# Moving four FP32 matmuls from ahead of a value chunk into three waits of the same chain

## The chip, the cores and the metric

One core of one Trainium2 chip. The metric is the device time of one execution of the whole kernel in microseconds (us). A run gives one such time; where a kernel ran several times, its median stands with its lowest and highest. Spans and the times inside a trace count from the first instruction of the profiled execution and end about 1.7 us below the device time of the same execution (667.5 against 669.24 for the kernel before). In the lines of the profile PE is the tensor engine (TensorE), PEld its weight loads, DVE VectorE, ACT ScalarE and SP the engine that issues the DMAs; L634 is line 634 of the kernel.

All runs of this study count as one state; no run was more than 1.5% above the fastest of its kernel. Below that limit the executions differ by more than the change can give (668.22 to 669.44 us over 48 runs of the kernel before), and much of this document is about that.

## The reference

A block of attention with a key and value cache, followed by a two-layer MLP, both with a modulated layer norm. Batch 8, one query position, D = 512, 32 query heads on 8 key heads of 128, 8,192 cached positions, F = 1,792, all bf16. The code here is condensed.

```python
def _A_ref(x, k_cache, v_cache, wq, wo):            # attention
    q = (x @ wq).reshape(B, Sq, Hq, Dh).transpose(0, 2, 1, 3)
    k, v = jnp.repeat(k_cache, rep, axis=1), jnp.repeat(v_cache, rep, axis=1)
    p = _softmax(jnp.einsum('bhqd,bhkd->bhqk', q, k) * Dh ** (-0.5))
    o = jnp.einsum('bhqk,bhkd->bhqd', p, v)
    return o.transpose(0, 2, 1, 3).reshape(B, Sq, Hq * Dh) @ wo
def _B_ref(x, w1, b1, w2, b2):                      # MLP
    h = jnp.einsum('bsd,df->bsf', x, w1) + b1
    r = jnp.where(h > 0, h, 0)
    return jnp.einsum('bsf,fd->bsd', r * r, w2) + b2
...                                                  # sa, ca, ga, sb, cb, gb from c and w_mod
h = _layernorm(x) * (1 + ca) + sa
x = x + ga * _A_ref(h, k_cache, v_cache, wq, wo)
h = _layernorm(x) * (1 + cb) + sb
x = x + gb * _B_ref(h, w1, b1, w2, b2)
```

## The kernel before

For each of the 8 batches the kernel reads four key units and four value units of 4 MB through a ring of four slots. Only the end matters here. The very last value unit comes in chunks, and the MLP weights follow it on the same queue, `w1` in two parts and `w2` in four:

```python
d_w1 = [dma("sync", s_w1[i], ...) for i, (a, z) in enumerate(((0, 3), (3, 4)))]
d_w2 = [dma("sync", s_w2[i], ...)
        for i, (a, z, j) in enumerate(((0, 4, 4), (4, 8, 4), (8, 12, 4), (12, 14, 2)))]
```

Most of the output projection is done early, before the last value unit is complete, in four column groups of the PE array. Their four partial sums must be added; that is done by `partial`, four FP32 matmuls with a selection matrix, into the same PSUM tile in which the last quarter of the projection is summed later:

```python
def partial(ks):
    for k in ks:
        op("tensor", lambda e, k=k: e.matmul(
            attn_ps[:, k, :], proj[:, 128 * k:128 * (k + 1)], SELP[:, :],
            start=(k == 0), stop=False, skip_group_check=True), [k_proj])
...
k_proj = op("vector", lambda e: e.tensor_copy(proj, bank(7)), [proj_done])
... # biases of the MLP (L704, L707)
partial(range(0, 4))                                               # L697, the group
t = values(16, CH[1] // 4, 22)                                     # L634, second chunk
osb = O_sb[:, 1, :]
t = op("vector", lambda e: e.tensor_copy(osb, bank(3)), [t])       # L713, the cast
direct(CH[1], CH[2], 2)                                            # L690 x16, third chunk
for i in range(4):
    op("tensor", ... e.matmul(oT_ps, osb[:, i * 128:(i + 1) * 128], SEL[:, i, :], ...), [t, k_all])   # L716
t = direct(CH[2], CH[3], 3)                                        # L690 x8, fourth chunk
t = op("vector", ... e.tensor_tensor(oTn_p[...], oT_ps, rinv_p[...], ALU.mult), [t])  # L720, the division
k_oP = permute(...)                                                # L522 and four copies
for g in (6, 7): ...                                               # L727, rest of the projection
```

After that come the residual, the second layer norm, the first MLP layer (L754) and the second (L769). L769 is 56 matmuls in order; from the 33rd on they read the third part of `w2`, from the 49th on the fourth. Line numbers after the change are higher by 2 to 4: L634 becomes L636, L690 L692, L697 L699, L716 L718, L727 L731, L754 L758, L769 L773.

Of the kernel before, what the change touches and what calls it, by code (L numbers as in the profile page):

```python
# [33 lines left out]
class Prog:  # L34
# [19 lines left out]
    def op(self, eng, fn, deps=()):  # L54
        o = Op(eng, fn, deps, None, self.at)
        o.tok = Tok(o, self.at)
        self.ops[eng].append(o)
        return o.tok
# [110 lines left out]
def bass_adaLN_cond__gqa_block_cached__dense_activation_squared_relu__decode_kernel(  # L169
# [17 lines left out]
    with ExitStack() as es:  # L187
# [67 lines left out]
        oP = KF[:, 3008:3072].rearrange("p (g j b) -> p g j b", g=2, j=4)  # L255
# [11 lines left out]
        bank = lambda i: PS[:, i, :]  # L267
# [40 lines left out]
        t = pool(lambda e: e.memset(SELB[:], 0.0))  # L308
# [6 lines left out]
        t = select(IDENT[:], [[-1, 128]], 0, 1, 1.0, NE, t)  # L315
        t = select(IDF8[:], [[-1, 8]], 0, 1, 1.0, NE, t)
# [3 lines left out]
        t = pool(lambda e: e.memset(EYEB[:], 0.0))  # L320
        t = select(EYE[:], [[-32, 4], [-1, B]], 0, 1, 1.0, NE, t)
        t = k_eye = select(EYEB[:], [[-32, 4], [-1, B]], 0, 1, 1.0, NE, t)
        k_q0 = pool(lambda e: e.memset(QTm[:], 0.0))
        t = pool(lambda e: e.memset(Pm[:], 0.0), [t])
        k_pm = t
        for d in (-96, -64, -32, 0, 32, 64, 96):
            t = select(R4[:], [[-1, 128]], -d, 1, 1.0, NE, t)
        t = select(Qmask[:], [[-32, 4]], 0, 1, 0.0, GE, t)
        t = select(Qmask[:], [[32, 4]], 31, -1, 0.0, GE, t)
        for d in (0, 32, 64, 96):  # L330
            t = select(R4m[:], [[-1, 32]], -d, 1, 0.5, NE, t)

        for i in range(4):
            for cg in range(4):
                for half in range(2):
                    t = select(SEL[:, i, 4 * half:4 * half + 4], [[-1, 4]], -(32 * cg + 8 * i + 4 * half), 1,
                               1.0, NE, t)

        t = pool(lambda e: e.memset(SELP[:], 0.0), [t])
        for j in range(4):  # L340
            t = select(SELP[:], [[-1, B]], -40 * j, 1, 1.0, NE, t)
        t = select(PERM[:], [[-1, 4], [0, 4], [-4, 32]], 0, 1, 1.0, NE, t)
        t = select(SELB[:], [[-1, 4], [0, B]], 0, 1, 1.0, NE, t)
        t = pool(lambda e: e.memset(oTn[:], 0.0), [t])
# [31 lines left out]
        for k in range(KT):  # L376
            t = op("tensor", lambda e, k=k: e.matmul(csT_ps[:, k, :], cs_k[:, k, :], IDENT[0:B, 0:B],
                                                    is_transpose=True), [k_cs, k_id])
# [3 lines left out]
        for k in range(KT):  # L382
            t = op("tensor", lambda e, k=k: e.matmul(xT_ps[:, k, :], x_sb[:, k * 128:(k + 1) * 128],
                                                    IDENT[0:B, 0:B], is_transpose=True), [d_x])
        k_xT = op("vector", lambda e: e.tensor_copy(xT[:], xT_ps), [t])
        t = op("vector", lambda e: e.bn_stats(stats[:], x_sb), [d_x])
        t = op("vector", lambda e: e.bn_aggr(mv[:], stats[:]), [t])
        t = op("vector", lambda e: e.tensor_scalar(std_[:], mv[:, 1:2], EPS, None, ALU.add), [t])
        t = op("scalar", lambda e: e.activation(std_[:], std_[:], ACT.Sqrt), [t])
        t = op("vector", lambda e: e.reciprocal(rstd[:], std_[:]), [t])  # L390
        t = op("vector", lambda e: e.tensor_scalar(hn, x_sb, mv[:, 0:1], rstd[:, 0:1], ALU.subtract, ALU.mult), [t])
# [18 lines left out]
        t = row_groups(bank(0), csT, wmod_v, (0, 1), [k_csT, d_wm])  # L410
        k_mr0 = op("vector", lambda e: e.tensor_copy(mod_r[0:64, 0, :], bank(0)[0:64, :]), [t])
        t = row_groups(bank(1), csT, wmod_v, (2, 3, 4, 5), [])
        released[2] = t
        k_mr1 = op("scalar", lambda e: e.activation(mod_r[:, 1, :], bank(1), ACT.Copy), [t])
        for i in range(KT):
            t = op("tensor", lambda e, i=i: e.matmul(
                mod_ab[:, :, i, :], mod_r[0:64, 0, :].rearrange("r (p i) -> r i p", i=KT)[:, i, :],
                EYE[0:64, 0:2, :]), [k_mr0, k_xT])
# [51 lines left out]
        def pe_stream(n, at):  # L470
            rhs = IDENT[:, :].unsqueeze(1).to_broadcast([128, 4, 128])
            ts = [op("tensor", lambda e: e.matmul(  # L472
                bank(at).rearrange("p (a r) -> p a r", a=4), IDENT[:, :], rhs)) for _ in range(n)]
            return ts[0]
# [41 lines left out]
        hT_ps = [bank(i)[:, 0:16 * n].rearrange("p (f a b) -> p f a b", f=n, a=2) for i, n in enumerate((8, FT - 8))]  # L516
        yT_ps = bank(2)[:, 0:KT * B].rearrange("p (k b) -> p k b", k=KT)

        def permute(pP, q0, q1, dst, deps, fill):
            n = q1 - q0  # L520
            for j in range(4):
                t = t_act = op("tensor", lambda e, j=j: e.matmul(  # L522
                    pP[:, j, 0:64 * n].rearrange("p (h x) -> p h x", h=2), PERM[:, j, :, :].rearrange("p h m -> p (h m)"),
                    oTn_p[:, :, q0:q1, :, :].rearrange("p h q r b -> p h (q r b)"), start=True, stop=True), deps)
            if fill:
                t_act = pe_stream(fill, 4)
            toks = []
            for hl in range(REP):
                rows = slice(32 * hl, 32 * (hl + 1))
                dst_h = dst[rows, :, :, :]  # L530
                frm = pP[rows, :, 0:64 * n].rearrange("p j (x r b) -> p r x j b", x=2 * n, b=B)[:, hl]
                if hl % 2:
                    toks.append(op("scalar", lambda e, dst=dst_h, frm=frm: e.activation(dst, frm, ACT.Copy), [t_act]))  # L533
                else:
                    toks.append(op("vector", lambda e, dst=dst_h, frm=frm: e.tensor_copy(dst, frm), [t]))
            return toks
# [10 lines left out]
        for b in range(B):  # L547
# [76 lines left out]
            for p in range(NP):  # L624
# [47 lines left out]
                else:  # L672
# [15 lines left out]
                    def direct(a, z, i):  # L688
                        for m in range(a, z):
                            t = op("tensor", lambda e, m=m: e.matmul(  # L690
                                oT_w, vt[:, m, :], wide(lhs[:, NP - 1, 8 * m:8 * m + 8]), start=(m == CH[1]),
                                stop=(m == CH[3] - 1), skip_group_check=True), [got[i], k_rinv] + pmd[m // 32])  # L692
                        return t
# [8 lines that stand above are left out]
                    for hh, (f0, n, a, z) in enumerate(((0, 4, 0, 2), (0, 4, 2, 3), (4, 2, 3, 4))):  # L702
# [4 lines left out]
                    op("tensor", lambda e: e.matmul(  # L707
                        yT_ps, b2_row, SELB[:, :, :], start=True, stop=False, skip_group_check=True),
                        [s_bank_free[2]])
                    partial(range(0, 4))  # L710
                    t = values(16, CH[1] // 4, 22)
                    osb = O_sb[:, 1, :]
                    t = op("vector", lambda e: e.tensor_copy(osb, bank(3)), [t])  # L713
                    direct(CH[1], CH[2], 2)
                    for i in range(4):
                        op("tensor", lambda e, i=i: e.matmul(  # L716
                            oT_ps, osb[:, i * 128:(i + 1) * 128], SEL[:, i, :], start=False, stop=False,
                            skip_group_check=True), [t, k_all])  # L718
                    t = direct(CH[2], CH[3], 3)
                    t = op("vector", lambda e: e.tensor_tensor(  # L720
                        oTn_p[:, :, NP - 1, :, B - 1], oT_ps.rearrange("p (h r) -> p h r", h=2),
                        rinv_p[:, :, NP - 1, :], ALU.mult), [t])
                    k_oP = permute(bank(6)[:, 0:256].rearrange("p (j c) -> p j c", c=64), 3, 4, oP, [t], 0)
                    for g in (6, 7):
                        for j in range(4):
                            for k in range(KT):
# [97 lines left out]
```

## Time and profile before

| kernel before, first runs | |
|---|---|
| time, 3 runs | 668.8 us (668.22 to 669.38) |
| time of the profiled execution | 669.24 us, span 667.5 us |
| mean granted PE clock in it | 0.915 |
| the group (L697) | 8 records on PE, 0.99 us |
| last transfer lands (fourth part of `w2`) | 663.63, which is 3.88 us before the end of the span |

"Lands" is the semaphore record of the last of the 16 DMA engines of a transfer. A PE clock of 0.5 is half of the full one; the FP32 loads of the moved matmuls then follow each other at 0.21 us instead of 0.11, as read below. The lines are shown in the prediction, where each is read. One row should be kept in mind: the profiled execution took 669.24 us, above two of the three runs, and I took its trace for the kernel as it usually is.

### The profile page before, as it was taken

How to read it: one execution, taken by the hardware profiler on the slowest of the kernel's cores; microseconds unless marked ns; L12 is line 12 of the kernel's file. 1: busy time of each engine (PE TensorE's matmuls, PEld its weight loads, DVE VectorE, ACT ScalarE, POOL GpSimd, SP SyncE). 2: the span in 40 equal slices, each digit the busy share in tenths (PEclk: the TensorE clock that was granted, in tenths of full speed). 3: DMA queues.
4: the chain of work that ended last, by engine and by line, in shares of the span. 5: the costliest groups of instructions: out<-in, count | busy, mean ns of one | idle time of the engine just before them, and what ended most of it. 6: DMA issues, size and time to landing. Idle time of an engine off the chain costs nothing.

```text
span 667.5 us, 15923 instructions
## 1 busy us (share of the span) xinstructions
PE 524.1 (79%) x7259; PEld 351.0 (53%) x7259; DVE 308.1 (46%) x587; ACT 264.6 (40%) x307; POOL 20.5 (3%) x79
## 2 busy tenths in 40 slices
PE   3309988899839987599758988499776998489886
PEld 2107753675328742477316753287434773177535
DVE  2105662566316652267415662167513673146633
ACT  2104661466105651166314661156512663146611
POOL 7400000000000000000000000000000000000000
PEclk9658999899969999699998999799996999979996
DMA  9999999999999999999999999999999999999996
GB/s 374 438 408 438 431 418 433 436 432 426 434 434 432 428 434 434 430 430 434 434 430 428 436 434 428 430 436 432 428 432 436 430 428 434 436 430 426 434 419 263
DMA packets 12188, 283.85 MB, mean 425 GB/s; under 512 B 1260, under 2 KB 1296, under 8 KB 3600
## 3 DMA queue, kind: packets, MB, share of 16 engines
q1 hardware_dynamic: 12128, 283.65, 99.1%
q8 instruction: 9, 0.15, 0.1%
q10 hardware_dynamic: 48, 0.02, 0.0%
q14 instruction: 3, 0.02, 0.0%
HBM read 283.66 MB, written 0.01 MB: 425 GB/s over the span
## 4 chain that ended last, share of the span: by engine, by line
PE 59%; DMA 29%; ACT 7%; DVE 3%; issue 1%; POOL 0%; ACTq 0%; SPq 0%; DVEq 0%; POOLq 0%
PE PS L488 39%; DMA ring<-in_A_k_cache_dram 22%; PE PS L505 10%; DMA wo_sb<-in_A_wo_dram 7%; ACT P_sb L580 5%; PE PS L634 4%; PE PS L478 2%; ACT KTb L493 1%; DVE O_sb L654 1%; PE PS L472 1%; PE PS L592 1%; DVE Pm L606 1%; PE PS L612 0%; PE PS L541 0%; PE PS L658 0%
## 5 line engine op out<-in xcount | busy, mean ns | idle before, releaser
L488 PE MATMUL PS<-IDENT,ring 128*128 128x128 bf16 x4096 | 266.4, 227 | 64.6 <-DMA ring<-in_A_k_cache_dram 37.0
L488 PEld LDWEIGHTS PS<-IDENT,ring 128*128 128x128 bf16 x4096 | 245.9, 102 | 112.8 <-issue 49.6
L493 ACT ACTIVATE KTb<-PS 128x1024 bf16<-128x1024 bf16 x192 | 196.8, 1025 | 237.6 <-PE PS L488 237.6
L495 DVE COPY KTb<-PS 128x1024 bf16<-128x1024 bf16 x320 | 210.0, 688 | 153.8 <-PE PS L488 151.8
L505 PE MATMUL PS<-KTb,Qb 128*32 128x512 bf16 x1024 | 78.8, 384 | 4.5 <-ACT KTb L493 4.5
L634 PE MATMUL PS<-ring,Pm 128*32 128x512 bf16 x1018 | 64.6, 396 | 20.8 <-DMA ring<-in_A_v_cache_dram 20.0
L654 DVE CAST O_sb<-PS 128x512 bf16<-128x512 f32 x31 | 21.4, 692 | 105.8 <-PE PS L634 105.8
L634 PEld LDWEIGHTS PS<-ring,Pm 128*32 128x32 bf16 x1018 | 26.1, 99 | 55.8 <-DMA ring<-in_A_v_cache_dram 28.4
L533 ACT ACTIVATE KTb<-PS 32x192 bf16<-32x192 f32 (+1 forms) x18 | 5.6, 311 | 109.9 <-PE PS L472 103.1
L580 ACT ACTIVATE P_sb<-PS,negm 128x1024 bf16<-128x1024 f32 x32 | 35.2, 1113 | 20.2 <-DVE negm L575 20.2
L478 PE MATMUL PS<-ONES 128*128 128x512 f32 x80 | 42.1, 630 | 0.0
L472 PE MATMUL PS<-IDENT 128*128 128x512 bf16 x112 | 33.4, 380 | 0.0
L592 PE MATMUL PS<-IDENT,P_sb 128*128 128x128 bf16 x256 | 19.9, 220 | 15.4 <-ACT P_sb L580 15.4
L606 DVE COPY Pm<-PS 64x512 bf16<-64x512 bf16 x48 | 20.2, 421 | 25.0 <-PE PS L592 24.6
L592 PEld LDWEIGHTS PS<-IDENT,P_sb 128*128 128x128 bf16 x256 | 14.4, 98 | 25.2 <-ACT P_sb L580 25.2
L505 PEld LDWEIGHTS PS<-KTb,Qb 128*32 128x32 bf16 x1024 | 15.4, 94 | 21.0 <-ACT KTb L493 8.5
L512 DVE TENSOR_REDUCE m<-PS 128x1 f32<-128x512 f32 x32 | 22.1, 689 | 6.6 <-PE PS L505 6.6
L658 PEld LDWEIGHTS PS<-SEL,O_sb 128*128 128x128 bf16 x124 | 5.8, 97 | 29.4 <-DVE O_sb L654 29.4
L478 PEld LDWEIGHTS PS<-ONES 128*128 128x128 f32 x80 | 12.7, 190 | 10.6 <-issue 10.6
L658 PE MATMUL PS<-SEL,O_sb 128*128 128x8 bf16 x124 | 7.9, 169 | 12.3 <-DVE O_sb L654 12.0
L472 PEld LDWEIGHTS PS<-IDENT 128*128 128x128 bf16 x112 | 9.9, 103 | 10.1 <-issue 7.2
L541 PE MATMUL PS<-wo_sb,KTb 128*32 128x512 bf16 x192 | 11.8, 380 | 3.4 <-ACT KTb L533 3.4
(134 smaller groups left out, 146.5 us busy)
## 6 DMA issues: line engine op xcount, KB each, us to landing
ring<-in_A_k_cache_dram SPq DMA_DIRECT2D x32, 4096.0 KB, 31.4
ring<-in_A_v_cache_dram SPq DMA_DIRECT2D x31, 4096.0 KB, 27.5
ring<-in_A_wq_dram SPq DMA_DIRECT2D x1, 4096.0 KB, 19.8
wo_sb<-in_A_wo_dram SPq DMA_DIRECT2D x1, 4096.0 KB, 46.7
ring<-in_w_mod_dram SPq DMA_DIRECT2D x1, 3072.0 KB, 10.5
ring<-in_A_v_cache_dram SPq DMA_DIRECT2D x1, 2048.0 KB, 22.3
ring<-in_B_w_dram SPq DMA_DIRECT2D x3, 512.0 KB, 19.1
ring<-in_B_w_dram SPq DMA_DIRECT2D x1, 1344.0 KB, 17.6
```

Source lines behind the costliest of these rows:

```text
L472: ts = [op("tensor", lambda e: e.matmul(bank(at).rearrange("p (a r) -> p a r", a=4), IDENT[:, :], rhs)) for _ in range(n)]
L478: ts = [op("tensor", lambda e: e.matmul(bank(at).rearrange("p (a r) -> p a r", a=4), ONES[:, :], rhs)) for _ in range(n)]
L488: t = op("tensor", lambda e, j=j, i=i: e.matmul(STG[j][:, i, :], src[:, 32 * k + 8 * j + i, :], IDENT[:, :], is_transpose=True), [loaded[n ...
L493: stg_free[j] = op("scalar", lambda e, j=j, dst=dst: e.activation(dst, STG[j], ACT.Copy), [t])
L495: stg_free[j] = op("vector", lambda e, j=j, dst=dst: e.tensor_copy(dst, STG[j]), [t])
L505: t = op("tensor", lambda e, hf=hf, q=q, rhs=rhs: e.matmul(PS[32 * q:32 * (q + 1), k, :], Qb[:, 2 * p + hf, :], rhs, start=(p == 0 and hf ...
L512: return op("vector", lambda e: e.tensor_reduce(m4[:, k:k + 1], bank(k), AX.X, ALU.max), [t])
L580: exps.append(op("scalar", lambda e, k=k: e.activation(P_sb[:, k, :, :, :], bank(k).rearrange("p (i x) -> p i x", i=8).unsqueeze(2).to_bro ...
L592: t = op("tensor", lambda e, k=k, i=i: e.matmul(STG[k][:, i, :], P_sb[:, k, i, :, :].rearrange("p h x -> p (h x)"), IDENT[:, :], is_transp ...
L606: done.append(op("vector", lambda e, dst=dst, frm=frm: e.tensor_copy(dst, frm), [t, k_pm]))
L634: t = op("tensor", lambda e, m=m, cg=cg, p=p, vt=vt, Obank=Obank: e.matmul(Obank[32 * cg:32 * (cg + 1), :], lhs[:, p, 32 * m:32 * m + 32], ...
L654: t = op("vector", lambda e, osb=osb, Obank=Obank: e.tensor_copy(osb, Obank), [t])
```

## The change

The four matmuls of `partial` are taken away from in front of the last unit's second chunk. One is put behind the issue of the cast, one behind the fourth chunk's matmuls (while the division runs), two behind the permutation's matmuls (while its four copies run). The intent is that PE does them while it waits for VectorE and ScalarE anyway.

```diff
-        def permute(pP, q0, q1, dst, deps, fill):
+        def permute(pP, q0, q1, dst, deps, fill, then=None):
...
+            if then is not None:
+                then()
             toks = []
...
-                    partial(range(0, 4))
                     t = values(16, CH[1] // 4, 22)
                     osb = O_sb[:, 1, :]
                     t = op("vector", lambda e: e.tensor_copy(osb, bank(3)), [t])
+                    partial((0,))
                     direct(CH[1], CH[2], 2)
...
                     t = direct(CH[2], CH[3], 3)
+                    partial((1,))
                     t = op("vector", lambda e: e.tensor_tensor(
...
-                    k_oP = permute(bank(6)[:, 0:256].rearrange("p (j c) -> p j c", c=64), 3, 4, oP, [t], 0)
+                    k_oP = permute(bank(6)[:, 0:256].rearrange("p (j c) -> p j c", c=64), 3, 4, oP, [t], 0,
+                                   lambda: partial((2, 3)))
```

> **What bounds the kernel now.** I read the page first, then the end in the chain of waits, then the weight loads and the DMA queue in order of time. From the page:
>
> ```profile
> span 667.5 us, 15923 instructions
> DMA  9999999999999999999999999999999999999996
> ...
> L634 PE MATMUL PS<-ring,Pm 128*32 128x512 bf16 x1018 | 64.6, 396 | 20.8 <-DMA ring<-in_A_v_cache_dram 20.0
> ```
>
> The 16 DMA engines are busy in all 40 slices but the last, and the value matmuls (L634) idle almost only for the value cache's transfers. The eight passes are bound by what they read; the instructions at issue run once, after the last pass. So the question is what sets the end. The chain of waits, from 651 to 666 us:
>
> ```profile
> 652.97 0.99 PE PS L697 x8
> 653.96 0.77 PE PS L634 x10
> 654.73 0.02 issue
> 654.75 0.70 DVE O_sb L713
> 655.46 0.05 issue
> 655.50 0.26 PE PS L716 x4
> 655.76 0.23 PE PS L690 x8
> ...
> 656.01 0.20 DVE oTn L720
> 656.21 0.05 issue
> 656.25 0.30 PE PS L522 x4
> ...
> 657.18 1.01 PE PS L727 x32
> ...
> 662.86 1.66 PE PS L769 x56
> ```
>
> L697 is the group to be moved. It stands on this chain with 0.99 us, and everything after it follows in one line of compute; no DMA is named. But a chain names only what was last. How long before that the data had landed is not in it, so I took each transfer's issue and its time to landing from the queue's timeline and the DMA view, one short window each:
>
> ```profile
> 627.73 0.43 SPq L364 DMA_DIRECT2D ring<-in_A_v_cache_dram  x1
> ring<-in_A_v_cache_dram SPq DMA_DIRECT2D x1, 1280.0 KB, 25.2
> ...
> 628.69 0.42 SPq L364 DMA_DIRECT2D ring<-in_A_v_cache_dram  x1
> ring<-in_A_v_cache_dram SPq DMA_DIRECT2D x1, 256.0 KB, 26.1
> ...
> 648.55 1.60 SPq L680 DMA_DIRECT2D ring<-in_B_w_dram  x1
> ring<-in_B_w_dram SPq DMA_DIRECT2D x1, 512.0 KB, 14.4
> ...
> 650.21 0.88 SPq L680 DMA_DIRECT2D ring<-in_B_w_dram  x1
> ring<-in_B_w_dram SPq DMA_DIRECT2D x1, 256.0 KB, 13.4
> ```
>
> Start of issue plus time to landing: the value unit's second chunk lands at 627.73 + 25.2 = 652.9 us (652.88 in the trace's semaphore records, which have two decimals; I use those below), the fourth at 654.8 (654.75), the third part of the second MLP weight at 663.0 (663.00), its fourth and last at 663.6 (663.63). By the same reading the third chunk lands at 654.06 and the first MLP weight at 658.09 and 659.23. The users come very shortly after, as the weight loads show:
>
> ```profile
> 653.88 0.33 PEld L634 LDWEIGHTS PS<-ring,Pm 128*32 128x32 bf16 x10
> 655.59 0.27 PEld L690 LDWEIGHTS PS<-Pm,ring 128*128 128x128 bf16 x8
> ```
>
> The reader should set 653.88 against 652.88, and 655.59 against 654.75: the stream of data and the stream of compute run side by side here, compute less than 1 us behind.
>
> [...] the first L634 load stands at 653.88, right after the last L697 load (653.67 + 0.19), although its data was there at 652.88. So program order is what is paid for, and moving the group moves its time. [...] an L697 load (128x128 f32) takes 0.19 us and the loads follow each other at 0.11 us, those of L690 (bf16) take 0.096 us and follow at 0.025 us. [...] the trace has two records for each of the four matmuls (x8)[...]. [...] The four matmuls keep their order [...]; correctness can only be seen in the run.
>
> **The change part by part.** It adds no work and removes none: four FP32 matmuls (8 records) are placed one after L634, one after L690's last, two after L522. The vector and scalar instructions and transfers are the same. Ahead of L634 the eight records hold PE from 652.90 (first load) to 653.88 = 0.99 us; that is what is offered. In their new places:
> (a) The first (2 records: one step of 0.11 us and the last load, 0.21 us until the next bf16 load = 0.32 us) goes under the cast L713, 0.69 us. Before, 16 L690 loads at 0.025 us = 0.4 us ran there and PE then idled 0.29 us.
> (b) The second, 0.32 us, goes between the last L690 load (655.77) and the first L522 load (656.25), a gap of 0.48 us while L720 works. Fits.
> (c) The last two (3 x 0.11 + 0.21 = 0.54 us) go between L522's last load (656.32) and L727's first (657.15), 0.83 us while the four copies work. Fits.
> So the new places are free, with 0.16 us to spare at the least. Now the walk with landings. What a landing costs to the load it frees I take from a true wait earlier: landed 499.07, load at 499.11, so 0.04 us.
> 1. L634 may load at 652.88 + 0.04 = 652.93 instead of 653.88: gain 0.96 us, nearly all.
> 2. Cast ends 0.96 earlier, at 654.49. The first moved matmul follows the last L634 load and ends its hold at about 654.0; L690's sixteen need the third chunk, 654.06 + 0.04 = 654.10, and are through at 654.5. L716 can start at 654.54, when the cast allows. Gain still 0.96.
> 3. L690's last eight would start at 654.63 but need the fourth chunk: 654.75 + 0.04 = 654.79 against 655.59. Gain cut to 0.80.
> 4. L720, L522, copies, L727, the layer norm and L754 keep 0.80. L754 would load at 658.66, its weight is there at 658.09 and 659.23 (the last quarter is used from 660.25). L769 starts at 662.06 instead of 662.86.
> 5. L769's 56 loads run at 0.027 us. Its 33rd stood at 663.71, its 49th at 664.14. With a gain of 0.80 they would stand at 662.91 and 663.34, but the third weight part is there at 663.04 and the fourth at 663.67. Gain cut to 0.67 and then to 664.14 - 663.67 = 0.47.
> 6. What follows is fixed work: the last eight matmuls, the gate, the residual, output.
> Sum: 0.99 offered, 0.03 + 0.16 + 0.33 = 0.52 taken by three landings, **0.47 us** left, 0.07% of 668.8. Predicted time 668.8 - 0.5 = **668.3 us**.
>
> **The rivals.**
> A. The whole 0.99 us comes through (667.8). For it: the chain names no DMA at the end. Against it: the landings above. It holds only if the transfers end earlier in the new kernel, and nothing in the change moves an issue: the MLP weights wait for L658 of an earlier value unit, at 640.3.
> B. The new places aren't free and the chain takes back part (668.3 to 668.8). For it: place (b) has only 0.16 us to spare, and FP32 loads at half clock take longer (L750, 0.29 us each instead of 0.19). The granted clock falls to 0.50 at 656.84 in this trace, after place (c) in the new schedule, but that moment need not be the same in every execution. [...] Against it: the 0.33 us that the last landing takes anyway would hide that.
> C. The landing itself differs between executions, so that either all or nothing of the gain shows. The three times of before are spread over 1.16 us, more than twice the gain, so a median of three may lie on either side.
> D. A clock that is lost earlier[...]. The tail's small matmuls hardly notice: L716 at full clock is spaced 0.026 us, L727 at half clock 0.026 us. [...]
>
> **Range and chances.** Median expected at 668.3. The walk gives 667.8 at best and 668.8 if all is lost; the spread of before, about 0.6 us to each side, and the state of another chip come on top: 667.5 to 669.1 should hold it 8 times in 10. Two per cent are 13.4 us, more than ten times what the moved instructions last[...]. Faster 0.005, same 0.99, slower 0.005.
>
> **What would show it right or wrong.** Right: in the weight loads of the new trace L634's second group starts within 0.1 us of the second chunk's landing; L690's last eight follow the fourth chunk by some 0.04 us and now name a DMA or stand idle before; L727 starts about 0.8 us earlier against the landings; L769 has a hole before its 33rd or 49th load, and the chain of waits holds a DMA of the MLP weight. The moved matmuls lie inside the waits, and L716, L522 and L727 follow their vector instruction by the same 0.05 to 0.1 us as now. Wrong: L769 runs unbroken and the end comes 0.8 us or more earlier (rival A: landings moved); L522 or L727 start late behind an FP32 load (B); or a span change that the tail, measured from the last landing, does not show (C).

No cut passage held a term of the sum: it came to 0.99 - 0.52 = 0.47 us and 668.3 us, as printed. That program order is what is paid for rests on the trace alone (the first L634 load at 653.88, with its data there at 652.88 and the last L697 load at 653.67). That the moved matmuls leave the attention sum in PSUM unchanged was argued in a cut passage and not shown. In rival B an estimate of the author's without its source is cut, 0.96 us for place (c) at half clock; the two L750 loads named there took 0.29 and 0.33 us. Rival D keeps only that a clock may be lost earlier; its cause and size were not shown. As to the state of another chip, named in the range: the medians of the kernel before on the five chips of the experiments were 668.49 to 668.74 us (on one of them of a single run).

## The result, and the profile after

| | before | after |
|---|---|---|
| time, 4 runs of each | 668.6 us (668.22 to 669.38) | 669.1 us (668.54 to 670.2) |
| ratio of fast runs, 95% interval | | 1.0008 (0.9991 to 1.0025) |
| profiled execution | 669.24 us, span 667.5 | 668.7 us, span 667.0 |
| last `w2` part lands, and from there to the end | 663.63, 3.88 us | 663.56, 3.42 us |

A ratio is the mean time of one kernel's fast runs over that of the other's of the same rounds, so not quite the ratio of the medians quoted here. No difference is shown: the interval includes 1. The predicted 668.3 lies 0.8 us below the median, which is at the very edge of the range (667.5 to 669.1), and two of the four runs are beyond it. Yet the profiled execution is 0.54 us shorter than that of before, nearly the 0.47 predicted. (That this is in part luck comes out below: the trace of before is of a rare kind.)

From the page of the changed kernel:

```profile
span 667.0 us, 15923 instructions
...
L636 PE MATMUL PS<-ring,Pm 128*32 128x512 bf16 x1018 | 66.5, 405 | 23.5 <-DMA ring<-in_A_v_cache_dram 22.7
```

The same number of instructions, and value matmuls that still idle almost only for their transfers: nothing has changed ahead of the end. The chain of waits near the end (start, duration, what):

```profile
627.31 26.67 DMA ring<-in_A_v_cache_dram
653.98 0.05 issue
654.02 0.57 PE PS L692 x16
...
654.71 0.36 PE PS L692 x8
655.08 0.30 PE PS L699 x2
655.38 0.38 PE PS L522 x4
655.76 0.81 PE PS L699 x4
656.57 0.86 PE PS L731 x32
...
662.11 1.87 PE PS L773 x56
```

The group's 0.99 us ahead of the second chunk is gone, and a DMA, the third value chunk, now stands in the chain. The moved records (L699) still stand in it, but inside what were waits. The weight loads of the same execution (start, duration, operation, count; in brackets idle time before and its releaser):

```profile
652.75 0.33 PEld L636 LDWEIGHTS PS<-ring,Pm 128*32 128x32 bf16 x10 [0.41 <-DMA ring<-in_A_v_cache_dram]
654.02 0.47 PEld L692 LDWEIGHTS PS<-Pm,ring 128*128 128x128 bf16 x16 [0.22 <-DMA ring<-in_A_v_cache_dram]
654.71 0.26 PEld L692 LDWEIGHTS PS<-Pm,ring 128*128 128x128 bf16 x8
655.36 0.24 PEld L522 LDWEIGHTS PS<-oTn,PERM 128*128 128x128 bf16 x4
655.52 0.96 PEld L699 LDWEIGHTS PS<-SELP,KTb 128*128 128x128 f32 x4
656.37 0.96 PEld L731 LDWEIGHTS PS<-KTb,wo_sb 128*128 128x128 bf16 x32
```

The chunks landed at 652.70, 653.98 and 654.67; the loads that they free start at 652.75, 654.02 and 654.71: 0.04 to 0.05 us behind each, as the prediction's walk has it. L731 starts at 656.37, 1.70 us after the fourth chunk landed; before, L727 started 2.40 us after (657.15 and 654.75). That is a gain of 0.70 where 0.80 was expected. Here the half clock begins at 655.08: L522's four matmuls hold the chain for 0.38 us instead of 0.30, and the last pair of moved matmuls (their FP32 loads 0.21 us apart instead of 0.11) ends close to where the copies do (656.26). In the first of the single looks below, where the half clock begins only at 657.20, L731 starts 1.59 us after the fourth chunk's landing, a gain of 0.81, so the predicted one. L773 starts at 662.11. Its 33rd load stands at 663.03 and its 49th at 663.60, each behind a hole, and the parts of `w2` landed at 662.93 and 663.56. So at the end the last landing sets the time: from it to the end are 3.42 us, 0.46 less than before.

All of this has the form of the predicted mechanism at close to the predicted size. What doesn't fit is the times: two of the four runs, 669.49 and 670.2, lie above every run of before.

### The profile page after: what moved, and what is told of

It reads as the page before. It is cut to its first block, busy times and chain, and to the rows that moved or that the text cites. A ratio compares the mean times of both kernels' runs of the same rounds, so it can differ in the third digit from the quotient of the medians.

```text
span 667.0 us, 15923 instructions
## 1 busy us (share of the span) xinstructions
PE 523.9 (79%) x7259; PEld 349.1 (52%) x7259; DVE 307.6 (46%) x587; ACT 264.4 (40%) x307; POOL 20.6 (3%) x79
## 4 chain that ended last, share of the span: by engine, by line
PE 54%; DMA 36%; ACT 6%; DVE 2%; issue 1%; POOL 0%; SPq 0%; POOLq 0%; DVEq 0%
PE PS L488 37%; DMA ring<-in_A_k_cache_dram 25%; PE PS L505 10%; DMA wo_sb<-in_A_wo_dram 7%; ACT P_sb L582 5%; DMA ring<-in_A_v_cache_dram 4%; PE PS L636 2%; PE PS L478 1%; ACT KTb L493 1%; DVE O_sb L656 1%; PE PS L472 1%; PE PS L594 1%; DVE Pm L608 0%; PE PS L614 0%; PE PS L773 0%
## 5 line engine op out<-in xcount | busy, mean ns | idle before, releaser
L488 PE MATMUL PS<-IDENT,ring 128*128 128x128 bf16 x4096 | 262.4, 225 | 63.1 <-DMA ring<-in_A_k_cache_dram 35.7
L488 PEld LDWEIGHTS PS<-IDENT,ring 128*128 128x128 bf16 x4096 | 241.9, 101 | 111.4 <-issue 48.1
L636 PE MATMUL PS<-ring,Pm 128*32 128x512 bf16 x1018 | 66.5, 405 | 23.5 <-DMA ring<-in_A_v_cache_dram 22.7
L505 PE MATMUL PS<-KTb,Qb 128*32 128x512 bf16 x1024 | 78.8, 384 | 4.5 <-ACT KTb L493 4.5
L505 PEld LDWEIGHTS PS<-KTb,Qb 128*32 128x32 bf16 x1024 | 15.4, 94 | 21.0 <-ACT KTb L493 8.5
```

The source lines that it names most:

```text
L488: t = op("tensor", lambda e, j=j, i=i: e.matmul(STG[j][:, i, :], src[:, 32 * k + 8 * j + i, :], IDENT[:, :], is_transpose=True), [loaded[n ...
L505: t = op("tensor", lambda e, hf=hf, q=q, rhs=rhs: e.matmul(PS[32 * q:32 * (q + 1), k, :], Qb[:, 2 * p + hf, :], rhs, start=(p == 0 and hf ...
L636: t = op("tensor", lambda e, m=m, cg=cg, p=p, vt=vt, Obank=Obank: e.matmul(Obank[32 * cg:32 * (cg + 1), :], lhs[:, p, 32 * m:32 * m + 32], ...
```

## The experiments

Three theories stood at the start, and a fourth was formed on the way.

1. The landing theory (that of the prediction): 0.47 us per execution, hidden in noise.
2. No gain in most executions: the trace of before shows an execution that was slow for another reason, and in the ordinary one the last landing already sets the end.
3. The moved matmuls cost something in some executions (clock, waits).
4. (After the second batch.) The shorter chain makes the transfer of the last weight part itself land late in some executions.

### Repeats on one chip: the changed kernel and the kernel before

The changed kernel and the kernel before, unaltered, five rounds each, beside nine runs of before on the same chip.

> The changed kernel, unaltered, over more rounds. Theory T (the end is 0.45 us shorter, and what differs between executions, over 1 us, is when the transfers land, not the end): in the new trace the span's end is 3.4 us after the last part of the second MLP weight has landed (3.44 in the first trace of this kernel, 3.88 in that of before), within 0.1; the ratio of times is 0.9993 within 0.001. Rival N (the change costs about 0.5 us, as the first median suggests): ratio at or above 1.0005 and an end of 3.9 us or more after the last landing in some execution. Rival F (the whole 0.99 us comes through): ratio 0.9985, no hole in the loads of the second MLP weight.

> The kernel before, submitted as if it were a change, as a null test. Theory T: ratio 1 within 0.001, with executions spread over 1 to 1.7 us although nothing differs, and an end 3.88 us after the last landing, within 0.1. If the ratio of equal kernels misses 1 by 0.0008 or more, the ratio 1.0008 of the change says nothing. Rival N needs the equal kernels to agree to within 0.0003 (0.2 us).

Before beside them: 668.49 (668.24 to 668.9). The changed kernel: 669.44, in two clusters, 668.55 and 668.56 against 669.44, 669.84 and 669.91; ratio 1.0014 (1.0000 to 1.0027). The unchanged one: 668.57 (668.34 to 669.44), ratio 1.0004 (0.9990 to 1.0018). The prediction's 668.3 is no better borne out here than at first. In the changed kernel's trace the end comes 3.41 us after the last landing, as the first theory had it; the ratio that it gave, 0.9993 within 0.001, is missed.

The trace of the unchanged kernel (668.34 us) tells more. Its weight loads:

```profile
651.92 0.97 PEld L697 LDWEIGHTS PS<-SELP,KTb 128*128 128x128 f32 x8
652.90 0.33 PEld L634 LDWEIGHTS PS<-ring,Pm 128*32 128x32 bf16 x10
...
654.61 0.27 PEld L690 LDWEIGHTS PS<-Pm,ring 128*128 128x128 bf16 x8
...
661.86 1.57 PEld L769 LDWEIGHTS PS<-KTb,ring 128*128 128x128 bf16 x56 [1.09 <-DVE KTb L764]
```

Here the group begins at 651.92 and the second chunk lands at 652.22, so the first third of the group lies ahead of the landing: L634 is 0.68 us behind its data, not 1.00. L690's last eight are 0.43 us behind their chunk (654.18), not 0.84. And L769's 56 loads run without a hole, yet the 49th starts at 663.14 with the last part of `w2` landed at 663.09, 0.05 us behind: compute and transfer meet there. In the first trace of before it was 0.51 us behind. The end comes 3.42 us after the last landing, just as in the changed kernel. In this execution there is nothing to gain.

What goes with the delay of the first trace is seen further up, in the last pass. In the windows view, over the same 2.7 us of both traces of before (window, its length, busy us and count of PE, PEld, DVE, ACT and POOL, granted PE clock, DMA share, GB/s), first the execution of 669.24 us:

```profile
589.20:591.90 2.70, 2.70 (x28) 2.70 (x27) 1.40 (x3) 1.17 (x2) 0.00 (x0) 0.50 0.99 425
```

and the one of 668.34 us:

```profile
589.20:591.90 2.70, 2.70 (x48) 2.17 (x46) 2.22 (x4) 1.66 (x2) 0.00 (x0) 1.00 0.93 400
```

At a clock of 0.50 PE does 28 matmuls in the time of 48 (most of them of L488 in both; eight of the 48 are wider ones of L505). The half clock lasts from 581.7 to 592.0 in the first and from 582.3 to 589.2 in the second, three and two times 3.41 us. The other stretches of half clock in the trace of before, up to the one that runs past the end, have lengths of 3.41, 6.83, 10.24 and 13.65 us and one of 27.31, all multiples of 3.41. Where the half clock falls differs between executions, and the traces show what goes with it: the last batch's third value unit starts 0.46 us after its landing in the first trace and 0.04 us after it in the second. All 20 traces of the study line up, whatever the kernel: the 13 in which the half clock ended at 590.5 or before start that unit 0.04 us behind its landing, the four in which it ended between 591.0 and 591.3 are 0.13 to 0.31 us behind, and the three in which it ended between 591.6 and 592.0 are 0.46 to 0.58 behind. The last three are called late below, the others ordinary. No run moved the half clock on purpose, so this is a relation seen in 20 traces and not an experiment. It also doesn't explain the whole difference of the two traces: their spans differ by 1.00 us, of which 0.46 lies after the last landing and 0.54 in a later landing (663.63 against 663.09), whose cause is open; the two other late traces, of other kernels, have it at 663.23 and 663.29.

### Without the group, and with the group twice

Without it the sum lacks the early part of the projection, a wrong result on purpose (the comparison with the reference passed all the same, so it does not see this part, and that the changed kernel passes it says little of the moved matmuls). Twice adds four equal matmuls into unused columns of the same bank.

```diff
# without
-                    partial(range(0, 4))
-   start=False, stop=(g == 7 and j == 3)
+   start=(g == 6 and j == 0 and k == 0), stop=(g == 7 and j == 3)
# twice
                     partial(range(0, 4))
+                    for k in range(4):
+                        op("tensor", lambda e, k=k: e.matmul(
+                            bank(4)[:, 32 + 8 * k:40 + 8 * k], proj[:, 128 * k:128 * (k + 1)], SELP[:, :],
+                            start=False, stop=False, skip_group_check=True), [k_proj])
```

> The kernel before with the four FP32 matmuls taken out and the attention sum started by the first of the later matmuls; wrong result on purpose, as the early projection is lost. Theory T: taking the work away is worth no more than moving it, since the landings cap both: end 3.44 us after the last landing, and 12.33 us after the fourth value chunk's (as in the changed kernel; before 12.76), within 0.1. Rival P (the moved matmuls cost something in their new places): this kernel ends 0.2 us or more earlier against the landings than the changed one.

> The kernel before with the group of four run twice ahead of the second chunk, the second time into unused columns of the same bank; right result. Theory T: at that place the group is wholly on the chain, so another 0.9 us (8 records at 0.11 us) is added: the end comes 4.8 us after the last landing and 13.65 us after the fourth value chunk's, ratio 1.0013. Rival H (the group was hidden by the landings there already): end unchanged at 3.88 us.

Without the group: 668.64 (668.46 to 668.8), ratio 1.0002 (0.9988 to 1.0015). So even taking the whole 0.99 us away shows no gain beyond the noise, and no place that the group is moved to should give more than that. Its trace happens to be a late one (half clock to 591.7, the third value unit 0.54 us behind its landing), and still the end comes 3.42 us after the last landing. So in a late execution the group costs 3.88 - 3.42 = 0.46 us (one trace against one), and in an ordinary one 0. Twice: 669.52 (669.08 to 670.11), ratio 1.0013 (0.9999 to 1.0027). The loads:

```profile
652.55 0.97 PEld L697 LDWEIGHTS PS<-SELP,KTb 128*128 128x128 f32 x8
653.43 0.97 PEld L712 LDWEIGHTS PS<-SELP,KTb 128*128 128x128 f32 x8
```

The second group follows 0.88 us behind the first, and the end comes 4.65 us after the last landing instead of 3.42. So the added group is paid in full (0.88) and 0.35 us more, which I did not separate. The first theory's size falls for ordinary executions, the second theory stands: the first group lies just where compute and landing meet, and one more does not.

### Four single looks on another chip

Three of the changed kernel and one of before, to see the second cluster in a trace.

> The changed kernel, unaltered, one more execution with a trace. Its nine executions so far fall into two groups, 668.5 to 668.7 us and 669.4 to 670.2 us, and both traces are of the first. Theory M [...]: which group an execution falls into is set by where the 3.41 us clock windows fall in the last pass: in a slow one the half clock lasts 3.4 or 6.8 us longer between 575 and 592 us, or falls within the tail's long matmuls (before 653.5 us), and the last key unit is worked off over 1 us later against the landings. Theory L (landings): in a slow one the last landings are 0.7 us or more later than 663.6 us, and the end is 3.4 us after them all the same. Theory N (the new places cost): a slow one has the same landings and the same key phase, and loses 1 us between the second chunk's matmuls and the first weight of the attention projection.

> As the look before: another execution of the changed kernel, to catch one of the slow group (669.4 us and more) with a trace. Theory M: half clock longer or earlier; theory L: later landings, end still 3.4 us after them; theory N: neither, and the time lost around the moved matmuls.

> As the looks before: a third execution of the changed kernel, the same three theories and their marks.

> The kernel before, another execution with a trace. Its first trace was of an execution of 669.24 us, its second of 668.34 us. Theory M: an execution near 668.4 has the short half clock in the last pass (6.8 us), its last value unit but one starts within 0.05 us of its landing, and it ends 3.4 us after the last landing, so the group of four is hidden in it; one near 669.3 has the long half clock (10 us), that unit starts 0.4 us or more late, and it ends 3.9 us after the last landing. Theory L: both end at the same distance from the last landing.

668.47, 669.62 and 668.49 us for the changed kernel, 668.46 for before. The look at before is an ordinary execution: the 49th load of L769 stands 0.04 us behind the last landing (663.23), and the end 3.42 us after it. The second look at the changed kernel fell into the upper cluster. L773's loads, of the first look:

```profile
661.62 0.94 PEld L773 LDWEIGHTS PS<-KTb,ring 128*128 128x128 bf16 x32 [1.08 <-DVE KTb L768]
662.71 0.86 PEld L773 LDWEIGHTS PS<-KTb,ring 128*128 128x128 bf16 x24 [0.16 <-issue]
```

and of the second:

```profile
661.37 0.94 PEld L773 LDWEIGHTS PS<-KTb,ring 128*128 128x128 bf16 x32 [1.08 <-DVE KTb L768]
662.51 0.51 PEld L773 LDWEIGHTS PS<-KTb,ring 128*128 128x128 bf16 x16 [0.20 <-issue]
664.52 0.29 PEld L773 LDWEIGHTS PS<-KTb,ring 128*128 128x128 bf16 x8 [1.51 <-DMA ring<-in_B_w_dram]
```

PE was 0.25 us earlier in the second, then its last eight loads waited 1.51 us for the weight. The chain of waits of that execution:

```profile
649.59 14.89 DMA ring<-in_B_w_dram
664.48 0.05 issue
664.53 0.38 PE PS L773 x8
```

The last part of `w2` landed at 664.48, 2.08 us after the third part. In the first look it was 663.24, 0.63 us after. From the landing to the end are 3.41 us in both. So the upper cluster of the changed kernel, here at least, is one transfer that lands late. The end no longer hangs on PE at all, and the third theory falls for this execution. So does theory M. The half clock does last 10.2 us here between 575 and 592 (575.75 to 579.16 and 582.57 to 589.40), but it does so too, in the same two pieces, in the first trace of the changed kernel (668.7 us), and the third value unit starts 0.04 us behind its landing as in ordinary executions.

What held it is in the DMA packet records near the end (each row: start to end, size). The transfer's last data packet had ended by 662.61; what is late is the last of its four-byte packets. The trace of before has 1,257 of them and 1,263 semaphore records of DMAs, 16 records for each transfer of the caches and weights; the last four-byte packet before the landing of the fourth part of `w2` ends there at 663.21, the landing is at 663.63. I take them for the reports of completion and call them completion packets. In the second look 15 of the 16 records stood by 663.04. A fetch of instructions is a packet of the kind "instruction" on queue 8: the page of before counts nine, and its trace has them at 16,384 bytes and 0.9 to 1.1 us each, two of them near the end.

| | fetch of instructions, 16,384 bytes | last completion packet, 4 bytes | landing |
|---|---|---|---|
| first look (668.47 us) | 662.44 to 663.54 | 662.81 to 662.82 | 663.24 |
| second look (669.62 us) | 662.35 to 663.45 | 663.44 to 663.46 | 664.48 |

The profile's DMA view of the second look, from 663.4 to 663.5, has exactly this one packet:

```profile
DMA packets 1, 0.00 MB, mean 0 GB/s; under 512 B 1, under 2 KB 1, under 8 KB 1
```

Every trace that loads all of `w2` has one such fetch that starts between 662.04 and 662.47 and takes 1.1 us. (In the kernel that leaves out half of `w2`, told below, it comes at 660.28.) In all 18 traces of the study without the late landing, the records in nanoseconds show the fetch starting 3 to 4 ns from the end of a four-byte completion packet. In the second look (and in one more slow trace below) it starts 4 ns before the end of a 2,048-byte data packet instead, and a completion packet starts as the fetch ends. My reading is that the completion stood behind the fetch. It rests on these times alone: the trace doesn't name the engine of a packet, and no run tests it. The landing follows the packet's end by 1.02 us here and by 0.42 us elsewhere; why was not shown. This became the fourth theory.

### Is it an earlier end of the chain, or the places

Four kernels on a third chip: the changed one again; the changed one with its chain put back by 0.4 us through a vector copy of unused data ahead of the division; the one without the group but with eight small bf16 matmuls in its place, so that PE's program has as many instructions as before; and the changed one that reads only the first two parts of `w2` (wrong on purpose, relative error 0.08), so that the last landing can't set the end.

```diff
# delayed, on the changed kernel
                     partial((1,))
+                    op("vector", lambda e: e.tensor_copy(O_sb[:, 0, 0:256], bank(7)[:, 0:256]), [t])
# no group, filled
-                    partial(range(0, 4))
+                    for _ in range(8):
+                        op("tensor", lambda e: e.matmul(
+                            bank(4)[:, 64:72], IDENT[:, :], IDENT[:, 0:8],
+                            start=False, stop=False, skip_group_check=True), [k_proj])
...   # and the start flag as in the kernel without the group
# W2 cut, on the changed kernel
-   ((0, 4, 4), (4, 8, 4), (8, 12, 4), (12, 14, 2))
+   ((0, 4, 4), (4, 8, 4))
-   W2v[:, f, k * 128:(k + 1) * 128] ... d_w2[f // 4]
+   W2v[:, f % 8, k * 128:(k + 1) * 128] ... d_w2[f % 8 // 4]
```

> The changed kernel, unaltered, for the shares of its two groups. So far 6 of its 12 executions took 669.4 us or more, and 3 of 19 of before's. The one slow execution with a trace had the last part of the second MLP weight landed 2.1 us after the third (0.6 in all other traces), its completion written at the end of a 1.1 us packet of the instruction queue. Theory F (that instruction fetch gets ahead of the last weight transfer's completion more often when the tensor engine's tail runs earlier against the landings): 2 to 4 of 5 at 669.4 or more, the rest at 668.3 to 668.8. Theory R (the slow ones come by chance in any kernel): 0 or 1 of 5.

> The changed kernel with one vector copy of about 0.4 us set ahead of the division by the softmax sum in the last value unit, so that all that follows runs as late against the landings as in before; tensor instructions and their order are those of the changed kernel. Theory F: the slow group goes (0 or 1 of 5 at 669.4 or more) and the others stay at 668.3 to 668.8, as 0.4 us are hidden behind the last landing; the median falls below that of the changed kernel. Theory R or a cause in the instruction order alone: as many slow ones as in the changed kernel; if the delay is not hidden, the fast ones rise by up to 0.4.

> The kernel without the group (wrong result on purpose, as before), with eight 128x8 bf16 matmuls on the identity into unused columns in its place, some 0.2 us: timing near that of no group, but as many tensor instructions as before. Without them none of 5 executions was slow. Theory F, in the form that the fetch is asked for at a fixed instruction number: with the count restored and the tail early, the slow group comes back (2 or more of 5 at 669.4 or more). If it stays at 0 or 1 of 5, the count is not what matters.

> The changed kernel with the last two of the four transfers of the second MLP weight (0.75 MB) left out and the first eight tiles used twice; wrong result on purpose. Theory T: the last landing no longer holds the end, so it comes 11.95 us after the fourth value chunk's landing instead of 12.31, with no hole in that weight's loads; the time of the fast executions falls by 0.3 to 0.4 us to some 668.2. Theory F: with nothing left for the fetch to overtake in time no execution reaches 669.4. Rival (the end is bound by compute from the value chunk on): 12.31 us as before the cut.

| kernel | median (lowest to highest) | ratio, 95% | runs above 669.5 |
|---|---|---|---|
| before, same chip, 9 runs | 668.69 (668.3 to 669.07) | | 0 |
| changed, again | 668.92 (668.27 to 669.59) | 1.0008 (0.9994 to 1.0021) | 2 of 5 |
| delayed | 668.20 (668.13 to 668.79) | 0.9993 (0.9979 to 1.0007) | 0 of 5 |
| no group, filled | 668.45 (668.1 to 668.6) | 0.9996 (0.9983 to 1.0010) | 0 of 5 |
| W2 cut | 668.21 (667.97 to 668.21) | 0.9992 (0.9978 to 1.0005) | 0 of 5 |

The text of the changed kernel miscounts before: on record only one of its executions so far (669.44) had reached 669.4 us; three had reached 669.2. Its theory F expected 2 to 4 of 5 at 669.4 or more, and 2 of 5 came.

The cut kernel settles the cap. Its last loads run without a hole:

```profile
661.82 1.57 PEld L773 LDWEIGHTS PS<-KTb,ring 128*128 128x128 bf16 x56 [1.09 <-DVE KTb L768]
```

From the fourth value chunk's landing to its end are 11.90 us, against 12.30 in ordinary executions of the uncut changed kernel: the last weight landing takes some 0.4 us of what the moved group gives, here shown by taking it away. Its five runs are also the closest together (0.24 us). The filled kernel has PE's instruction count and an early chain (its last loads start at 661.43, earlier than in the first look), and no run in the upper cluster. So neither an early chain alone nor a fixed place in the program brings the cluster at the rate of the changed kernel, as far as five runs can tell: at a rate of 6 in 18, five runs would show none in 13 of 100 cases, and ten (these and the five without the group) in 2 of 100. The delayed kernel has the matmuls in the new places and the added 0.4 us: none either. Its trace shows no hole in L774's 56 loads from 662.33 on, and the end 3.51 us after the landing.

### Which places

On a fourth chip: two of the four matmuls back at the old place and one each under the cast and the division; two back and two in the copies' wait; the delayed kernel again; and one more look at the changed one. On a fifth: three back and one under the cast, or one under the division.

```diff
# under the cast and the division: at the old place, then at the cast, then at the division
+                    partial((0, 1))
-                    partial((0,))
+                    partial((2,))
-                    partial((1,))
+                    partial((3,))
-                                   lambda: partial((2, 3)))
# in the copies' wait: at the old place; the copies' wait keeps (2, 3)
+                    partial((0, 1))
-                    partial((0,))
-                    partial((1,))
# one under the cast (or, in the other kernel, under the division) only
+                    partial((0, 1, 2))
+                    partial((3,))
```

> Two of the four matmuls stay ahead of the second chunk, one runs under the cast and one under the division; none in the copies' wait. If the two in the copies' wait bring the slow executions: 0 or 1 of 5 at 669.2 us or more. If the other two places, or the early tail alone, bring them: 2 or more of 5. The fast ones at 668.2 to 668.8 either way, the end 3.4 us after the last landing.

> Two of the four matmuls stay ahead of the second chunk, the other two run in the wait for the four copies, as in the changed kernel. If these bring the slow executions: 2 or more of 5 at 669.2 us or more; otherwise 0 or 1. The fast ones at 668.2 to 668.8.

> The delayed version again. Its median was 668.2, 0.5 us under that of before on the same chip, without slow executions. If that holds: ratio 0.9993 within 0.0004, 0 or 1 of 5 at 669.2 us or more. If it was luck: a share of 2 or more of 5, or a median equal to that of before.

> Another traced execution of the changed kernel. If it is slow (669.2 us or more): theory F expects the last part of the second MLP weight to land 1.5 us or more after the third, at the end of a packet of the instruction queue, and a hole of over 1 us before the last eight matmuls on it. If it is fast: that part lands 0.6 us after the third.

> Three of the four matmuls stay ahead of the second chunk, one runs under the cast. If the place under the cast brings the slow executions: 2 or more of 5 at 669.2 us or more. Otherwise 0 or 1, and a median within 0.3 us of before on the same chip.

> Three of the four matmuls stay ahead of the second chunk, one runs between the last matmuls on the value chunk and the permutation, under the division. If this place brings the slow executions: 2 or more of 5 at 669.2 us or more. Otherwise 0 or 1, and a median within 0.3 us of before on the same chip. If neither this run nor the other has any, it takes both, or the earlier tail.

| kernel | median (lowest to highest) | ratio, 95% | runs above 669.5 |
|---|---|---|---|
| before, fourth chip, 9 runs | 668.58 (668.35 to 669.34) | | 0 |
| under the cast and the division | 669.76 (668.61 to 670.28) | 1.0010 (0.9996 to 1.0023) | 3 of 5 |
| in the copies' wait | 668.44 (668.2 to 668.63) | 0.9995 (0.9981 to 1.0009) | 0 of 5 |
| delayed, again | 668.45 (668.24 to 668.67) | 0.9995 (0.9982 to 1.0009) | 0 of 5 |
| changed, one look | 668.43 | | 0 of 1 |
| before, fifth chip, 9 runs | 668.74 (668.33 to 669.36) | | 0 |
| one under the cast | 668.6 (668.25 to 669.44) | 0.9998 (0.9985 to 1.0012) | 0 of 5 |
| one under the division | 668.84 (668.42 to 670.42) | 1.0007 (0.9993 to 1.0020) | 1 of 5 |

The profiled execution of the kernel under cast and division (669.83 us) is the second slow trace. Its last part of `w2` lands at 664.60, 2.25 us after the third; the fetch lasts from 662.47 to 663.58 and a completion packet from 663.56 to 663.59; L773's last eight loads wait 1.68 us for the DMA; and from the landing to the end are again 3.41 us. The same picture as in the second look, in another kernel, on another chip. The one look at the changed kernel is a fast execution, and its last part lands 0.64 us after the third.

So the cluster came with matmuls under the cast and the division together (3 of 5), and not with those in the copies' wait alone (0 of 5, which chance gives in 13 of 100 cases at the rate of the changed kernel): pointed to, not shown. For either of the first two places alone the runs decide nothing: 0 and 1 of 5. Over the whole study, runs above 669.5 us: 0 of 48 of the kernel before (highest 669.44), 6 of 18 of the changed kernel, 3 of 5 and 1 of 5 of the two variants named, and none of 35 of the other seven submissions that were timed in rounds (the one with the group twice is left out, as it does more work). The limit of 669.5 was chosen after seeing the runs. With the limits put on record beforehand the picture is the same, if less sharp: at 669.4 or more 1 of 48 of before and 8 of 18 of the changed kernel, at 669.2 or more 6 of 48 and 8 of 18, and the kernel with one matmul under the cast then has 1 of 5 (669.44). The mean granted clock does not tell the ten above 669.5 from the rest: it is 0.914 to 0.946 in them. There is one more reserve: only two of these ten executions have a trace; that the other eight have the same cause is inferred from their times.

Why those places raise the odds is open. Counted from the start of the span the fetch starts hardly later in the slow traces (662.35 and 662.47) than in some fast ones (662.38 and 662.44). Counted from the transfer it does: the last data packet of `w2` ends 0.26 and 0.08 us after the fetch has started in the two slow traces, and 0.35 to 1.04 us after it in the 17 others that load all of `w2`. So a late landing went with a fetch that met the very end of the transfer. With two traces this is a hint, and no run set that distance on purpose.

No version is shown to beat both kernels. The delayed one and the one with two matmuls in the copies' wait have the lowest medians of those that leave no work out, 668.20, 668.45 and 668.44, but their intervals all include 1.

## Why the prediction was wrong

**What was right.** The order of the program is what was paid for: without the group in front, the second chunk's load follows its landing by 0.05 us. The new places are free to within 0.1 us (L731 came 0.70 us earlier against the fourth chunk in one trace and 0.81 in another, with 0.80 expected; rival B, seen at its edge: the last pair did run at half clock in the first of these and barely fitted). The gain is cut by the landings and most of all by the last one: shown by the holes before L773's 33rd and 49th load, and by the cut kernel, where the holes go. Rival A falls with that. In the pair of traces that were profiled the end moved from 3.88 to 3.42 us after the last landing, 0.46 against the predicted 0.47. That this number came out is luck in part: it sets a late execution of before against an ordinary one of the changed kernel, and two ordinary ones (3.42 against 3.41) would have shown 0.01. One reading was off without consequence: under the cast PE is said to idle for 0.29 us, where the trace has 0.39, because the sixteen loads begin 0.11 us ahead of the cast.

**The step that failed first: the walk's step 5**, "Gain cut to 0.67 and then to 664.14 - 663.67 = 0.47". It subtracts a landing from a load of one trace, and I took that distance for the kernel's. It belongs to a late execution: 0.51 us in that trace, 0.05 and 0.04 us in the two other traces of before. In those the term is 0.01 or less once the 0.04 us of the landing's own delay is taken off, so no gain is left, and the ordinary runs say the same: those below 669.2 us have a mean of 668.59 for before (42 of 48) and 668.56 for the changed kernel (10 of 18; the limit was chosen after the runs). Two more traces fit: with three of the four matmuls in the old place the end comes 3.74 us after the last landing where the half clock ended at 591.9, and 3.47 where it ended at 591.1. Rival C came nearest ("either all or nothing of the gain shows"), but it gave the landing as the reason. The landings do differ (663.09, 663.23 and 663.63 for the last part in the three traces of before), but the end follows them. The distance between landing and load, which decides over the gain, goes with where PE's half clock ends: 592.0 in the first trace, 589.2 and 589.4 in the other two, some 75 us before the end. That the change saves the 0.46 us in a late execution is shown only for the kernel without the group; no trace of the changed kernel fell on one as late.

**The step that failed second: "nothing in the change moves an issue"**, and so the landings were taken as given. The issue times indeed moved no more than between executions of one kernel (the last one starts at 649.64 to 650.21 in three traces of before, at 649.59 to 650.12 in seven of the changed kernel). But in both traced slow executions the last part's completion came behind a fetch of instructions and landed 2.08 and 2.25 us behind the third part instead of 0.63, by which the execution lost some 1.2 us (span 667.9 against 666.7 in the other two looks on the same chip). The median of 669.1 is the mean of 668.7 and 669.49: two of the four runs lay high. Neither of these two has a trace, so that a late landing made them high is inferred.

**The range** took its spread from three runs of before, 0.6 us to each side. It had no room for a cluster that before does not have. The chances, 0.99 for within 2%, rested on the size of the moved work and held.

## What to carry to other kernels

When a gain is worked out from the distance between a landing and its user, take that distance from several traces of the kernel: here it was 0.51 us in one and 0.05 in two others, and the one profiled at first had a time above most of its own runs, which was the sign to ask for another. Where the last load of this kernel met its last compute to within 0.1 us (0.05 and 0.04 us in the two ordinary traces of before), a shorter compute chain had nothing to gain (ratio 1.0002 without the group), and the first thing to try is to take the work away altogether: the run without the group cost one kernel and shows what any move of it can give at most. And look at single times, not only at medians, before explaining a half-microsecond loss: two clusters 1.2 us apart need a trace from each.
